# A fused attention and spectral-mixing kernel: the last loop gets one PSUM bank per z tile, a new order of steps, other modes for its pairs, the batch ends at places 15 and 16, and a second store queue

## The chip, the core and the metric

The kernel runs on one core of a Trainium2 chip. The core has a matrix engine (TensorE, PE in the profile; PEld are its weight loads), VectorE (DVE), ScalarE (ACT), GpSimd (POOL) and SyncE (SP). Each takes its own instructions in program order; they meet through semaphores. TensorE writes its sums to PSUM, eight banks of 128 partitions by 512 fp32 values; results leave through ACT or DVE to SBUF, and go to memory by DMA. The metric is the device time of one execution in microseconds (us), the median over several runs.

## The reference

```
scores = q k^T / 8 + min(-(cum_i - cum_j), 0), causal;  cum = cumsum(max(s, 0))
attn = softmax(scores) v                       # 8 batches, 8 heads, 576 x 64
x = heads side by side                         # 8 x 576 x 512
X = rfft(x, axis=1);  Y[m] = X[m] (w_r + i w_i)[m]   # the first 64 modes, each 512 x 512
u = x + irfft(Y, n=576)
out = u + max(u @ w_ch, 0)                     # 8 x 576 x 512, fp32
```

## The kernel before

A first stage computes attention for one head pair and batch after the other, then the forward transform of its result as matrix products (`fft`), while the mode weights stream in through GpSimd's DMA queue. A second stage (`modes`, called for eight chunks `c` of eight modes each) multiplies the modes; each chunk gives `yb`, the spectral rows y, and with `w_ch` the rows `vb` = y w_ch. Because u = x + G y (G is the inverse transform), the product u w_ch is x w_ch + G (y w_ch). So `yv` holds, for each batch, the 128 spectral rows (16 for each chunk) of both kinds: `which` = 0 for y, 1 for y w_ch. A small DMA (`spread`, L491, on SP's queue) moves the rows of the last two chunks to their places in `yv`. The last chunk's rows are the last to arrive.

The last loop forms the output. Its unit is a pair of row tiles of 128 x 512 values: `pairs` lists 18 of them, 16 ordinary pairs (b, T), (b, T + 1) and two pairs of **batch ends**, the last 64 rows of each batch, four batches in a pair, two tiles of two times 64 rows. Before, these stand at places 2 and 4. For each pair two sums are formed in PSUM, each of two banks:

- u: step X (`add_x`, L749) puts x into it through an identity matrix, step U (`add_u`, `add_y`, L721) adds G y.
- z: step Z (`add_z`, `add_y`, L721) puts in G (y w_ch). The product x w_ch was made and kept in SBUF earlier (`z1s`), for all but the first two pairs. How it joins z is the pair's mode in `ways`: "s", ACT copies it into PSUM first (step S, `seed`, L872); "e", it is kept as two fp16 digits and added by four matmuls (step E, L878); "v", DVE adds it (step K, L784); "g", ACT copies z to SBUF and GpSimd adds it there (both in step R, L769 and L770). In the other modes R is ACT's relu from PSUM to the result tile `r_w` (L774).
- step F (`finish`, L792 or L794), on DVE, adds max(z, 0) and u, and issues the store on SP's queue (L796; for batch ends two stores of 64 partitions each, L801).

The z tiles come from `zpool`, two buffers of two banks; the u tiles from two pools, one for even and one for odd pairs. So X of pair i waits for F of pair i - 2, and a new z tile waits until both banks of the tile two before are read. All of it is scheduled by hand: the string of steps near the end is the order in which the instructions are emitted, and each engine takes its own in that order. Pairs 0 and 1 (`NPRE`) have their z nearly complete before the loop: chunk 6 and 7 are added with `add_last`, which takes y w_ch of one chunk straight from `vb`, with a matrix `Gx_sb` that holds that chunk's rows of G at the partitions of batch 0, and doesn't wait for the `spread`. For other pairs Z reads all 128 rows of `yv`.

```
if ways.get(i) == "g":
    nc.scalar.copy(out=rs[i], in_=zs[i])
    nc.gpsimd.tensor_tensor(out=rs[i], in0=rs[i], in1=z1s[i], op=ALU.add)
```

Of the kernel before, what the change touches and what calls it, by code (L numbers as in the profile page):

```python
# [18 lines left out]
def kernel(  # L19
# [60 lines left out]
    G_np = G_np.reshape(P, SP).astype(np.float16)  # L80
# [24 lines left out]
    G_sb = gp.tile([P, SP], FP16, name="G_sb")  # L105
# [391 lines left out]
    for i, b in ((2, 0), (4, B // 2)):  # L497
        pairs.insert(i, ((b, NF), (b + 2, NF)))
# [4 lines left out]
    ways = dict(zip(kept, "evgvggeggsgsgsgs"))  # L503
# [85 lines left out]
    zpool = ctx.enter_context(tc.tile_pool(name="z_psum", bufs=2, space=PSUM))  # L589
# [33 lines left out]

    def x_times_wch(i, last):
        zs[i] = z = zpool.tile([P, 2, DM], FP32, name="z_ps", tag="z")
        for x in range(2):
            for dt in range(DT):
                nc.tensor.matmul(  # L628
                    z[:, x, :], xts[i][:, x, dt, :], wch_sb[:, dt, :],
# [3 lines left out]
    def keep(i):  # L633
# [7 lines left out]
        keep_product(i, slice(0, 2), zs.pop(i))  # L641
# [72 lines left out]
    x_pool = ()  # L714
    GK = P - 2 * MC * NX

    def add_y(dst, i, which, rows=slice(0, P), start=False):

        for x, (b, T) in enumerate(pairs[i]):
# [7 lines left out]
    def add_last(dst, i, yb, cols=slice(0, DM), c=NX - 1):  # L727

        for x, (b, T) in enumerate(pairs[i]):
            nc.tensor.matmul(  # L730
                dst[x][:, cols], Gx_sb[:, c, bass.ts(T, P)], yb[:, cols],
                start=False, stop=True, skip_group_check=True,
            )
# [31 lines left out]
    def relu(i):  # L765

        rs[i] = result(i)
        if ways.get(i) == "g":
            nc.scalar.copy(out=rs[i], in_=zs[i])  # L769
            nc.gpsimd.tensor_tensor(out=rs[i], in0=rs[i], in1=z1s[i], op=ALU.add)  # L770
            return
        n = 1 if i in (0, last) else 2
        for x in range(0, 2, n):
            nc.scalar.activation(out=rs[i][:, x : x + n], in_=zs[i][:, x : x + n], func=ACTF.Relu)  # L774
        if i in x_pool:
            b, T = pairs[i][0]
            r = rs[i].rearrange("p x (g d) -> p x g d", d=P)
            nc.gpsimd.tensor_tensor(
                out=r, in0=r, in1=x_all[:, :, b, T : T + 2, :].rearrange("p g t d -> p t g d"), op=ALU.add
            )  # L780

    def kept_sum(i):
        rs[i] = result(i)
        nc.vector.tensor_tensor(out=rs[i], in0=zs[i], in1=z1s[i], op=ALU.add)  # L784

# [148 lines left out]
```

## Time and profile before

| | |
|---|---|
| median of 4 runs | 446.97 us (446.69 to 447.4) |
| the profiled execution | 447.04 us, its span 445.1 us |
| granted TensorE clock, mean | 0.912 |
| bytes written to memory | 9.44 MB |

The page cuts the span into 40 slices and gives for each the busy tenths of every engine and of the DMA engines. The last loop is the end of it:

| window, us | PE | DVE | ACT | POOL | DMA share | GB/s |
|---|---|---|---|---|---|---|
| 400 to 410 | 8.90 | 2.34 | 0.58 | 0.00 | 0.75 | 150 |
| 410 to 420 | 9.48 | 6.98 | 5.08 | 1.07 | 0.36 | 131 |
| 420 to 430 | 9.91 | 8.30 | 8.60 | 10.00 | 0.95 | 316 |
| 430 to 440 | 8.56 | 9.09 | 6.99 | 7.65 | 1.03 | 398 |
| 440 to 446 | 0.00 | 0.58 | 0.00 | 0.00 | 0.55 | 210 |

The columns are busy microseconds of each engine in the window, the mean busy share of the 16 DMA engines (which can come out a little over 1), and the rate at which they moved data. The last mode weights land at 408.5 us and the last matmul on them (L456) starts at 408.58 us; the first relu of the loop (L774) starts at 412.61 us. Of one execution's rows, these are the durations in the loop: two matmuls of 512 columns 0.59 us, and a matmul every 0.2155 us where many follow each other; an ACT step on 1024 columns 1.02 us (L769, L774, L872), on 512 columns 0.594 us; a DVE step on 1024 columns 1.22 us (L792, L794), on 512 columns 0.683 us; GpSimd's sum on 1024 columns (L770) 2.37 us.

### The profile page before, as it was taken

How to read it: one execution, taken by the hardware profiler on the slowest of the kernel's cores; microseconds unless marked ns; L12 is line 12 of the kernel's file. 1: busy time of each engine (PE TensorE's matmuls, PEld its weight loads, DVE VectorE, ACT ScalarE, POOL GpSimd, SP SyncE). 2: the span in 40 equal slices, each digit the busy share in tenths (PEclk: the TensorE clock that was granted, in tenths of full speed). 3: DMA queues.
4: the chain of work that ended last, by engine and by line, in shares of the span. 5: the costliest groups of instructions: out<-in, count | busy, mean ns of one | idle time of the engine just before them, and what ended most of it. 6: DMA issues, size and time to landing. Idle time of an engine off the chain costs nothing.

```text
span 445.1 us, 11399 instructions
## 1 busy us (share of the span) xinstructions
PE 341.0 (77%) x4697; PEld 217.2 (49%) x4729; DVE 251.2 (56%) x574; ACT 221.1 (50%) x387; POOL 243.0 (55%) x375
## 2 busy tenths in 40 slices
PE   1688998995909599892498759399987997768994
PEld 1366665563606365661366436256664555433341
DVE  7766766672605366671266527157765564451785
ACT  1576787464606375671256525256661244321593
POOL 7766656565556566455565546464644443530393
PEclk9998999996967889997579969889999799989998
DMA  9999999999999999999999999999999999996598
GB/s 181 201 207 206 204 206 204 208 206 207 207 209 202 206 202 183 205 206 208 207 202 206 208 207 203 209 206 203 203 210 209 211 210 209 209 217 133 179 351 334
DMA packets 72675, 93.30 MB, mean 210 GB/s; under 512 B 29664, under 2 KB 31200, under 8 KB 72624
## 3 DMA queue, kind: packets, MB, share of 16 engines
q0 software_dynamic: 63408, 81.29, 104.2%
q1 hardware_dynamic: 9216, 11.29, 7.8%
q8 instruction: 37, 0.61, 0.5%
q14 instruction: 14, 0.11, 0.1%
HBM read 163.51 MB, written 9.44 MB: 389 GB/s over the span
## 4 chain that ended last, share of the span: by engine, by line
DMA 55%; PE 22%; POOL 6%; DVE 6%; issue 5%; ACT 3%; POOLq 1%; DVEq 0%
DMA w_sb<-in_moe_w_r_dram 20%; DMA qk<-in_k_dram 19%; DMA w_sb<-in_moe_w_i_dram 14%; PE z_ps L628 4%; PE yp L456 4%; PE sc_ps L378 3%; POOL r_w L770 3%; PE tr_ps L336 3%; POOL w_sb L232 2%; PE sc_ps L372 2%; DMA x_all<-in_moe_w_r_dram 2%; ACT p_sb L386 1%; PE ft_ps L433 1%; PE av_ps L407 1%; PE xt_ps L618 1%
## 5 line engine op out<-in xcount | busy, mean ns | idle before, releaser
L386 ACT ACTIVATE p_sb<-sc_ps,cumt_sb 128x576 f16<-128x576 f32 (+1 forms) x256 | 141.6, 636 | 50.2 <-PE sc_ps L378 49.8
L232 POOL DMA_DIRECT2D w_sb<-in_moe_w_r_dram x120 | 71.2, 594 | 62.0 <-DMA w_sb<-in_moe_w_r_dram 17.0
L232 POOL DMA_DIRECT2D w_sb<-in_moe_w_i_dram x120 | 71.1, 594 | 62.1 <-DMA w_sb<-in_moe_w_i_dram 19.2
L340 DVE COPY qt<-tr_ps 64x576 bf16<-64x576 bf16 x64 | 47.8, 747 | 75.3 <-PE tr_ps L336 75.3
L336 PE MATMUL tr_ps<-ident,qk 64*64 64x64 bf16 x1152 | 34.9, 204 | 65.1 <-DMA qk<-in_k_dram 27.5
L378 PE MATMUL sc_ps<-qt,kt 128*128 128x64 bf16 (+2 forms) x352 | 69.9, 306 | 4.2 <-ACT kt L340 2.2
L232 POOL DMA_DIRECT2D v<-in_v_dram x72 | 52.1, 724 | 34.7 <-DMA w_sb<-in_moe_w_i_dram 10.0
L336 PEld LDWEIGHTS <-qk 64*64 64x64 bf16 x1152 | 26.5, 117 | 75.3 <-DMA qk<-in_k_dram 28.6
L372 PE MATMUL sc_ps<-negm,ident 128*128 128x256 bf16 x256 | 53.9, 295 | 0.2
L378 PEld LDWEIGHTS <-kt 128*128 128x128 bf16 x384 | 40.1, 105 | 26.2 <-issue 5.0
L357 ACT ACTIVATE p<-sc_ps,cumt 128x64 f16<-128x64 f32 x32 | 10.0, 314 | 72.1 <-PE sc_ps L353 72.1
L456 PE MATMUL yp<-w_sb,xs 128*32 128x512 bf16 (+1 forms) x480 | 38.6, 407 | 9.1 <-DMA w_sb<-in_moe_w_i_dram 2.6
L407 PE MATMUL av_ps<-v,p_sb 128*128 128x65 f16 x1024 | 43.3, 195 | 0.1
L407 PEld LDWEIGHTS <-p_sb 128*128 128x128 f16 x1024 | 37.7, 99 | 4.8 <-DVE x_all L417 1.9
L443 DVE CAST xs<-ft_ps 64x128 bf16<-64x128 f32 x128 | 31.4, 284 | 7.0 <-PE ft_ps L433 6.2
L412 DVE TENSOR_REDUCE den<-av_ps 128x5 f32<-128x10 f32 x64 | 10.8, 169 | 41.4 <-PE av_ps L407 40.4
L433 PE MATMUL ft_ps<-Ff_sb,x_all 128*64 128x96 f16 (+1 forms) x640 | 32.3, 220 | 1.0 <-DVE x_all L417 1.0
L417 DVE TENSOR_TENSOR x_all<-av_ps,rcp 128x320 f16<-128x320 f32 x64 | 31.4, 491 | 2.2
L456 PEld LDWEIGHTS <-xs 128*32 128x32 bf16 (+1 forms) x512 | 19.3, 145 | 23.3 <-issue 9.5
L340 ACT COPY kt<-tr_ps 64x576 bf16<-64x576 bf16 x32 | 23.0, 719 | 15.2 <-DVE qt L340 14.6
L433 PEld LDWEIGHTS <-x_all 128*64 128x64 f16 (+1 forms) x640 | 22.0, 111 | 8.8 <-DVE x_all L417 1.1
L628 PE MATMUL z_ps<-wch_sb,xs 128*128 128x512 f16 x96 | 24.9, 406 | 0.2 <-DVE xs L622 0.2
(111 smaller groups left out, 425.5 us busy)
## 6 DMA issues: line engine op xcount, KB each, us to landing
w_sb<-in_moe_w_r_dram POOLq DMA_DIRECT2D x120, 256.0 KB, 8.8
w_sb<-in_moe_w_i_dram POOLq DMA_DIRECT2D x117, 256.0 KB, 8.7
out_dram<-r_w SPq DMA_DIRECT2D x14, 512.0 KB, 3.2
v<-in_v_dram POOLq DMA_DIRECT2D x72, 64.0 KB, 7.4
qk<-in_q_dram POOLq DMA_DIRECT2D x15, 288.0 KB, 7.9
qk<-in_k_dram POOLq DMA_DIRECT2D x15, 288.0 KB, 9.2
x_all<-in_moe_w_i_dram POOLq DMA_DIRECT2D x6, 256.0 KB, 7.5
out_dram<-r_w SPq DMA_DIRECT2D x6, 256.0 KB, 3.2
```

What stands on the lines that cost most here:

```text
L232: nc.gpsimd.dma_start(out=dst, in_=src)
L336: nc.tensor.transpose(ps[rows, r, :], src[rows, r, :], ident16[rows, rows])
L340: copy(out=to[:, :, :, half * RH : half * RH + RH], in_=ps[HP * i : HP * i + HP].rearrange("d r (h p) -> d h p r", h=2),)
L372: nc.tensor.matmul(ps[:, bass.ds(w * S, W)], ident16, negm[:, bass.ts(r, W)], start=True, stop=False, skip_group_check=True,)
L378: nc.tensor.matmul(ps[:, c0 : c0 + i1 - i0], keys[:, w, r, :], qh[:, i0:i1], start=False, stop=True, skip_group_check=True,)
L386: nc.scalar.activation(out=pt[:, poff[x] : poff[x] + S - w * W], in_=ps[:, w * S : (w + 1) * S - w * W], func=ACTF.Exp, bias=cumt_sb[:, x, ...
L407: nc.tensor.matmul(ps[:, I, r : r + NCH], lhsT, rhs, start=(i == 0), stop=(i == len(todo) - 1), skip_group_check=True,)
L417: nc.vector.tensor_tensor(out=x_all[:, g, b, :, D * h : D * h + D], in0=ps[:, :, 1 : NCH], in1=rcp.unsqueeze(2).to_broadcast([P, NT, D]), ...
L433: nc.tensor.matmul(ps[HP * h : HP * h + HP, q_, :], x_all[:nT, g, b, T, q_::2], Ff_sb[:nT, T, 3 * HM * h : 3 * HM * (h + 1)], start=(T == ...
L443: nc.vector.tensor_copy(out=xs[g % 2][rows, :, k, h, :, b, :], in_=ps[rows, :, k * HM : (k + 2) * HM].rearrange("p q (r m) -> p q r m", r=2),)
L456: nc.tensor.matmul(ps[32 * cg : 32 * cg + 32, :], cols[k0:, q_, 1 - ri, :, c * MC // 2 + cg], wt[(g, c, ri, cg // 2)][k0:, 2 * (cg % 2) + ...
L628: nc.tensor.matmul(z[:, x, :], xts[i][:, x, dt, :], wch_sb[:, dt, :], start=(dt == 0), stop=(last and dt == DT - 1), skip_group_check=True,)
```

## The change

It touches the last loop, what leads to it, and which pair is handled where:

- z tiles are one bank each, named by the parity of the pair and the half: four tags with one buffer each. The steps S, E, Z, R and K are given for one half ("a" or "b"), and GpSimd's sum becomes a step of its own, G, also by halves. X, U and F stay whole, but F of pairs 0 and 17 is given by halves.
- The batch ends move to places 15 and 16. Pairs 2 to 14 are now ordinary pairs.
- `ways` changes: "g" holds for eight pairs as before (now 2, 4, 8, 10, 11, 13, 15, 17), "v" for 3 and 5 as before, "e" for one pair (7) in place of two, "s" for five (6, 9, 12, 14, 16) in place of four.
- Pair 2 (batch 1) is `direct`: its Z takes 112 rows from `yv`, and the last chunk's 16 rows from `vb` through a new matrix `Gy_sb`, which has that chunk's rows of G at the partitions of batch 1. `Gy_sb` is cleared by DVE and loaded by SP once, beside `Gx_sb`.
- Of each pair of batch ends the first store goes to SP's queue in F, the second to ACT's queue in a step D of its own.
- For pairs 0 and 1 the last chunk's sums are ordered by column halves first, then by pairs.
- `G_sb` is 576 columns wide in place of 640.
- The order of all steps is a new one.

```diff
--- before.py
+++ after.py
...
-    G_np = G_np.reshape(P, SP).astype(np.float16)
+    G_np = np.ascontiguousarray(G_np.reshape(P, SP)[:, :S].astype(np.float16))
...
-    G_sb = gp.tile([P, SP], FP16, name="G_sb")
+    G_sb = gp.tile([P, S], FP16, name="G_sb")
...
     pairs = [((b, T), (b, T + 1)) for b in range(B) for T in range(0, NF, 2)]
-    for i, b in ((2, 0), (4, B // 2)):
+    for i, b in ((15, 0), (16, B // 2)):
         pairs.insert(i, ((b, NF), (b + 2, NF)))
...
-    ways = dict(zip(kept, "evgvggeggsgsgsgs"))
+    ways = dict(zip(kept, "gvgvsegsggsgsgsg"))
...
-    zpool = ctx.enter_context(tc.tile_pool(name="z_psum", bufs=2, space=PSUM))
+    Gy_sb = finpool.tile([P, 2 * P], FP16, name="Gy_sb")
+    nc.vector.memset(Gy_sb.bitcast(FP32), 0.0)
+    nc.sync.dma_start(out=Gy_sb[1:P:B], in_=d_Gx[:, NX - 1, : 2 * P])
+    zpool = ctx.enter_context(tc.tile_pool(name="z_psum", bufs=1, space=PSUM))
...
+    def start_z(i, x):
+        zs[i, x] = zpool.tile([P, DM], FP32, name="z_ps", tag=f"z{i % 2}{x}")
+
     def x_times_wch(i, last):
-        zs[i] = z = zpool.tile([P, 2, DM], FP32, name="z_ps", tag="z")
         for x in range(2):
+            start_z(i, x)
             for dt in range(DT):
                 nc.tensor.matmul(
-                    z[:, x, :], xts[i][:, x, dt, :], wch_sb[:, dt, :],
+                    zs[i, x], xts[i][:, x, dt, :], wch_sb[:, dt, :],
                     start=(dt == 0), stop=(last and dt == DT - 1), skip_group_check=True,
...
-        keep_product(i, slice(0, 2), zs.pop(i))
+        for x in range(2):
+            keep_product(i, x, zs.pop((i, x)))
...
+    direct = (2,)
...
-    def add_y(dst, i, which, rows=slice(0, P), start=False):
-
-        for x, (b, T) in enumerate(pairs[i]):
+    def add_y(dst, i, which, rows=slice(0, P), start=False, xx=(0, 1)):
+
+        for x in xx:
+            b, T = pairs[i][x]
             for r, bb, _ in parts(b, T):
                 nc.tensor.matmul(
...
-    def add_last(dst, i, yb, cols=slice(0, DM), c=NX - 1):
-
-        for x, (b, T) in enumerate(pairs[i]):
+    def add_last(dst, i, yb, cols=slice(0, DM), c=NX - 1, xx=(0, 1)):
+
+        for x in xx:
+            b, T = pairs[i][x]
             nc.tensor.matmul(
-                dst[x][:, cols], Gx_sb[:, c, bass.ts(T, P)], yb[:, cols],
+                dst[x][:, cols], Gy_sb[:, bass.ts(T, P)] if b else Gx_sb[:, c, bass.ts(T, P)], yb[:, cols],
...
-    def relu(i):
-
-        rs[i] = result(i)
+    def relu(i, x):
+
+        if i not in rs:
+            rs[i] = result(i)
         if ways.get(i) == "g":
-            nc.scalar.copy(out=rs[i], in_=zs[i])
-            nc.gpsimd.tensor_tensor(out=rs[i], in0=rs[i], in1=z1s[i], op=ALU.add)
-            return
-        n = 1 if i in (0, last) else 2
-        for x in range(0, 2, n):
-            nc.scalar.activation(out=rs[i][:, x : x + n], in_=zs[i][:, x : x + n], func=ACTF.Relu)
-        if i in x_pool:
-            b, T = pairs[i][0]
-            r = rs[i].rearrange("p x (g d) -> p x g d", d=P)
-            nc.gpsimd.tensor_tensor(
-                out=r, in0=r, in1=x_all[:, :, b, T : T + 2, :].rearrange("p g t d -> p t g d"), op=ALU.add
-            )
-
-    def kept_sum(i):
-        rs[i] = result(i)
-        nc.vector.tensor_tensor(out=rs[i], in0=zs[i], in1=z1s[i], op=ALU.add)
-
-    def finish(i):
-        n = 1 if i in (0, last) else 2
+            nc.scalar.copy(out=rs[i][:, x], in_=zs[i, x])
+        else:
+            nc.scalar.activation(out=rs[i][:, x], in_=zs[i, x], func=ACTF.Relu)
+
+    def gpsimd_sum(i, x):
+
+        r = rs[i][:, x]
+        if ways.get(i) == "g":
+            nc.gpsimd.tensor_tensor(out=r, in0=r, in1=z1s[i][:, x], op=ALU.add)
+        else:
+            b, T = pairs[i][x]
+            r = r.rearrange("p (g d) -> p g d", d=P)
+            nc.gpsimd.tensor_tensor(out=r, in0=r, in1=x_all[:, :, b, T, :], op=ALU.add)
+
+    def kept_sum(i, x):
+        if i not in rs:
+            rs[i] = result(i)
+        nc.vector.tensor_tensor(out=rs[i][:, x], in0=zs[i, x], in1=z1s[i][:, x], op=ALU.add)
+
+    def finish(i, x=None):
+        xx = slice(0, 2) if x is None else slice(x, x + 1)
         b, T = pairs[i][0]
-        for x in range(0, 2, n):
-            o, u = rs[i][:, x : x + n, :], us[i][:, x : x + n, :]
-            if ways.get(i) in ("v", "g"):
-                nc.vector.scalar_tensor_tensor(out=o, in0=o, scalar=0.0, in1=u, op0=ALU.max, op1=ALU.add)
-            else:
-                nc.vector.tensor_tensor(out=o, in0=u, in1=o, op=ALU.add)
-            if T < NF:
-                nc.sync.dma_start(
-                    out=out[b, bass.ds((T + x) * P, n * P), :].rearrange("(x p) e -> p x e", p=P), in_=o
-                )
+        o, u = rs[i][:, xx, :], us[i][:, xx, :]
+        if ways.get(i) in ("v", "g"):
+            nc.vector.scalar_tensor_tensor(out=o, in0=o, scalar=0.0, in1=u, op0=ALU.max, op1=ALU.add)
+        else:
+            nc.vector.tensor_tensor(out=o, in0=u, in1=o, op=ALU.add)
         if T == NF:
-            for r, bb, _ in parts(b, T):
-                nc.sync.dma_start(
-                    out=out[bb : bb + 3 : 2, NF * P :, :].rearrange("x t e -> t x e"), in_=rs[i][r]
-                )
+            store_tails(nc.sync, i, 0)
+        else:
+            n = 2 if x is None else 1
+            nc.sync.dma_start(
+                out=out[b, bass.ds((T + (x or 0)) * P, n * P), :].rearrange("(x p) e -> p x e", p=P), in_=o
+            )
+
+    def store_tails(queue, i, y):
+        b, T = pairs[i][0]
+        r, bb, _ = parts(b, T)[y]
+        queue.dma_start(out=out[bb : bb + 3 : 2, NF * P :, :].rearrange("x t e -> t x e"), in_=rs[i][r])
 
     def z_of(i):
-        return [zs[i][:, x, :] for x in range(2)]
+        return [zs[i, x] for x in range(2)]
...
-    for i in range(NPRE):
-        for cols in halves:
+    for cols in halves:
+        for i in range(NPRE):
             add_last(z_of(i), i, vb, cols)
...
-    def start_z(i):
-        zs[i] = zpool.tile([P, 2, DM], FP32, name="z_ps", tag="z")
-
-    def seed(i):
-        start_z(i)
-        nc.scalar.copy(out=zs[i], in_=z1s[i])
-
-    def digits(i):
-        start_z(i)
-        for x in range(2):
-            for y in range(2):
-                nc.tensor.matmul(
-                    zs[i][:, x, :], ident16h, z1s[i][:, y, x, :],
-                    start=(y == 0), stop=False, skip_group_check=True,
-                )
-
-    def add_z(i):
-        if i not in zs:
-            start_z(i)
-        add_y(z_of(i), i, 1, start=ways[i] in ("v", "g"))
+    def seed(i, x):
+        start_z(i, x)
+        nc.scalar.copy(out=zs[i, x], in_=z1s[i][:, x])
+
+    def digits(i, x):
+        start_z(i, x)
+        for y in range(2):
+            nc.tensor.matmul(
+                zs[i, x], ident16h, z1s[i][:, y, x, :], start=(y == 0), stop=False, skip_group_check=True,
+            )
+
+    def add_z(i, x):
+        start = (i, x) not in zs
+        if start:
+            start_z(i, x)
+        z = {x: zs[i, x]}
+        if i in direct:
+            add_y(z, i, 1, slice(0, P - 2 * MC), start=start, xx=(x,))
+            add_last(z, i, vb, xx=(x,))
+        else:
+            add_y(z, i, 1, start=start, xx=(x,))
 
...
     steps = {
-        "S": seed, "E": digits, "Z": add_z, "R": relu, "K": kept_sum, "X": add_x, "U": add_u, "F": finish,
+        "S": seed, "E": digits, "Z": add_z, "R": relu, "G": gpsimd_sum, "K": kept_sum, "X": add_x, "U": add_u,
+        "F": finish, "D": lambda i: store_tails(nc.scalar, i, 1),
     }
     for step in (
-        "R0 X1 F0 U1 R1 E2 F1 Z2 Z3 R2 X2 K3 U2 Z4 F2 X3 R4 Z5 U3 K5 Z6 X4 R6 U4 F3 Z7 E8 R7 F4 Z8 X5 R8 "
-        "Z9 U5 R9 X6 F5 U6 Z10 S11 F6 X7 U7 R10 Z11 F7 X8 R11 U8 Z12 F8 X9 S13 U9 X10 R12 F9 Z13 U10 R13 "
-        "Z14 F10 X11 U11 S15 F11 X12 R14 U12 Z15 F12 X13 R15 U13 Z16 F13 X14 R16 U14 X15 F14 S17 U15 F15 "
-        "X16 U16 Z17 F16 X17 R17 U17 F17 "
+        "R0a X1 R0b U1 F0a R1a Z2a F0b Z2b R1b R2a X2 F1 U2 R2b G2a Z3a Z3b K3a Z4a Z4b R4a X3 G2b K3b Z5a "
+        "R4b U3 K5a S6a Z5b G4a S6b F2 E7a Z6a Z6b R6a G4b Z7a F3 X4 R6b U4 R7a Z8a K5b Z8b S9a X5 F4 U5 "
+        "R8a E7b R8b G8a Z7b F5 Z9a R7b X6 U6 R9a G8b Z10a S9b F6 X7 R10a U7 Z9b S12a G10a Z10b F7 X8 R9b "
+        "U8 R10b Z11a F8 Z11b S12b X9 G10b U9 R11a Z12a R11b F9 X10 G11a R12a U10 Z12b S14a Z13a F10 X11 "
+        "G11b R12b U11 R13a Z13b Z14a S14b F11 X12 G13a R14a U12 R13b Z14b Z15a F12 R14b X13 G13b U13 R15a "
+        "Z15b S16a X14 G15a F13 R15b U14 S16b Z16a Z17a R16a Z17b G15b F14 Z16b X15 R17a U15 R16b G17a X16 "
+        "R17b F15 U16 G17b F16 X17 D15 U17 F17a D16 F17b "
     ).split():
-        steps[step[0]](int(step[1:]))
+        i = int(step[1:].rstrip("ab"))
+        if step[-1] in "ab":
+            steps[step[0]](i, "ab".index(step[-1]))
+        else:
+            steps[step[0]](i)
```

## The prediction

> **What bounds the kernel now.** I read the page's slices first, then the chain of waits, then the last loop in the timeline and in windows of half a microsecond.
>
> ```profile
> POOL 7766656565556566455565546464644443530393
> DMA  9999999999999999999999999999999999996598
> GB/s 181 201 207 206 204 206 204 208 206 207 207 209 202 206 202 183 205 206 208 207 202 206 208 207 203 209 206 203 203 210 209 211 210 209 209 217 133 179 351 334
> ```
>
> For 36 of 40 slices the DMA engines are full with weights. The change leaves those bytes alone (`G_sb` is 128 bytes shorter in each partition: nothing), so I count the start of the loop as unmoved: the weight stream ends it at 408.6 us, and modes reordered behind it are hidden by the stream. Only slices 37 to 40 can change. There, the timeline of before (start, duration, engine, instruction, the idle time before it and what ended it):
>
> ```profile
> 415.10 1.16 PE L721 MATMUL z_ps<-yv,G_sb 128*64 128x512 f16 x6 [0.34 <-DMA yv<-v_sb]
> 418.71 1.35 SPq L801 DMA_DIRECT2D out_dram<-r_w  x2
> 418.93 2.37 POOL L770 TENSOR_TENSOR r_w<-r_w,r_sb 128x1024 f32<-128x1024 f32 x1 [20.18 <-ACT r_w L769]
> 421.26 14.17 POOL L770 TENSOR_TENSOR r_w<-r_w,z 128x1024 f32<-128x1024 f32 x6
> 430.62 1.22 DVE L792 SCALAR_TENSOR_TENSOR r_w<-r_w,u_ps 128x1024 f32<-128x1024 f32 x1 [0.52 <-POOL r_w L770]
> 439.30 1.28 DVE L794 TENSOR_TENSOR r_w<-u_ps,r_w 128x512 f32<-128x512 f32 x2
> ```
>
> GpSimd's first sum starts only at 418.93, because the first Z that reads `yv` waits for the spread until 415.10. From then GpSimd has hardly a gap: 8 x 2.37 = 18.96 us. DVE waits for it, last before the row at 430.62, which is F10 (the order of DVE's rows is the order of the F and K steps). The windows show what the chain of waits doesn't:
>
> ```profile
> 419.50:420.00 0.50, 0.50 (x5) 0.14 (x4) 0.50 (x2) 0.34 (x1) 0.50 (x1) 1.00 0.00 0
> 420.00:420.50 0.50, 0.50 (x6) 0.14 (x4) 0.50 (x2) 0.50 (x1) 0.50 (x1) 1.00 0.85 197
> 420.50:421.00 0.50, 0.50 (x6) 0.21 (x3) 0.50 (x1) 0.18 (x1) 0.50 (x1) 1.00 0.99 197
> 421.00:421.50 0.50, 0.50 (x4) 0.19 (x2) 0.32 (x2) 0.20 (x1) 0.50 (x2) 1.00 0.89 193
> 421.50:422.00 0.50, 0.50 (x4) 0.23 (x3) 0.50 (x1) 0.50 (x1) 0.50 (x1) 1.00 1.03 365
> ...
> 432.50:433.00 0.50, 0.50 (x4) 0.22 (x3) 0.48 (x1) 0.48 (x1) 0.41 (x1) 1.00 0.59 225
> 433.00:433.50 0.50, 0.50 (x4) 0.27 (x3) 0.49 (x1) 0.07 (x1) 0.44 (x1) 1.00 1.08 422
> ...
> 442.50:443.00 0.50, 0.00 (x0) 0.00 (x0) 0.00 (x0) 0.00 (x0) 0.00 (x0) 0.50 1.06 414
> 443.00:443.50 0.50, 0.00 (x0) 0.00 (x0) 0.00 (x0) 0.00 (x0) 0.00 (x0) 0.50 0.18 66
> ```
>
> The last three columns are clock, DMA share, GB/s. From 433 on the store engines are full, at about 406 GB/s: one pair (524,288 bytes) takes **1.29 us**. F10 ends at 431.84, its data flow 0.9 us later (432.75), and eight pairs are left: 432.75 + 8 x 1.29 = 443.07, where the windows show the data end at about 443.1. So the end is GpSimd, then F10, then **the stores**, not DVE's last row at 440.58; 2.0 us of landing and closing work follow to 445.1. A pair of batch ends is dear: from 420.05 it moves at 195 GB/s with full engines, then at 365, and 0.524 MB are through at about 422.15: **2.1 us** a pair. Summed over the windows, 0.29 MB are gone at 421.5, so the first half (64 partitions) takes 1.35 us and the second less.
>
> **The change, part by part.**
>
> **Direct pair 2 and the new order.** PE runs X1 and U1 from 412.73 (4 x 0.2155), then Z2 from 413.59, with no landing to wait for; the 0.34 us of PE at 415.10 goes. ACT takes R0 and R1 by halves from 412.5 (4 x 0.49, the step between two 512-column rows in sequence), then R2a to 415.1: GpSimd starts at 415.2 in place of 418.93. Pair 2's four added matmuls (0.86 us) stand where PE waited; the four of the lost "e" (0.86) go. What is late next: the sums themselves.
>
> **GpSimd by halves.** No row shows 512 columns. Below: half of 2.37, 1.19. Above: 1.6, if a fixed 0.8 us is in each. The Trainium skill (GPSIMD Engine Reference, section "Elementwise — side-by-side cycle accounting") gives 4.497 us for 2048 columns; with the row of 2.37 for 1024 a straight line gives 2.08 ns a column and 0.24 fixed, so I take the estimate 1.30. 16 x 1.30 = 20.8 against 18.96: by the row alone the halves are free, by the rule they cost 1.8 us of the 3.7 gained.
>
> **ACT and DVE.** ACT's halves: 0.98 a pair against 0.92 to 1.04 between whole rows, so nothing; one more seed is 0.98, inside the 1.4 us that ACT was idle between 420 and 430 (8.60 busy of ten). DVE: K by halves 4 x 0.61 against 2 x 1.22, nothing. F stays whole for 16 pairs.
>
> **Walking the new list.** I gave every step the durations above (PE 0.2155 a matmul and 0.375 for the last to come out; batch ends 0.5 for each four; DVE 1.16 in sequence; 0.04 to 0.09 from one engine to the next) and each engine its steps in order. The old list so walked has F10 ending at 432.00 (trace: 431.84) and F17 at 440.83 (trace: 440.58), so 0.2 is to be taken off. The new list: F4 421.9, F9 428.1, F13 433.7, F14 434.9, F15 436.5, F17b 438.9. F15 starts when U15's matmuls are out (X15 and U15, 1.0 us, behind Z16b), just after GpSimd's G15b. DVE ends **1.9 us earlier**.
>
> **Stores.** Fourteen ordinary pairs go first. F4's data can flow at 422.7, and eleven pairs (4 to 14) need 14.2 us: 436.9. So the queue is empty when F15 ends at 436.3 (436.5 less 0.2). The batch ends need about 1.3 us from issue to data (418.71 to 420.05): **437.65**. Left are two pairs of batch ends and pair 17, 1.29: the end of data is 437.65 + 2p + 1.29, p the time for one pair of batch ends. It equals the 443.1 of before at **p = 2.08**. D15 and D16 stand on ACT behind its last relu (R17b, 435.5), so nothing waits behind them; SP issues T15, T16, F17a, F17b in order and is free each time.
>
> **What two queues do for p.** Before, one after the other on SP, p is 2.1 (the row). If the halves fill each other's gaps, p is 1.29, the rate of a full tile. The Trainium skill speaks against it (SBUF — State Buffer, section "Can I just issue two DMAs to hit both halves?"): two concurrent DMAs on partitions 0 and 64 came out only 6% faster than in turn, since they share the same engines. With the first half's 1.35 for each this is 2.7 / 1.06 = 2.55, which the row of 2.1 already beats without a second queue. The trace has the second half partly at 365 GB/s, so the upper half isn't held to half the rate, and could pass while the lower waits. Nearest is the lower half alone, 1.35; I take **p = 1.5**, between it and the row, with 1.29 and 2.55 kept for the range.
>
> Sum: 437.65 + 3.0 + 1.29 = 441.94; less 443.1 is -1.16. 447.04 - 1.16 = 445.88 for the profiled execution; the median stands 0.07 below that execution, so **445.8**.
>
> **What was at nothing.** `Gy_sb`'s clear and load stand beside `Gx_sb`'s (0.485 us of DVE at 341.3, 0.498 of SP after it), 60 us before their first use, hidden by the weights; uncovered, half a microsecond each. The halves first order in `add_last` brings pair 1's z no later. F0a starts 0.07 earlier: it moves no store that binds.
>
> **Rivals** (0.2%, 0.9 us, is what a measurement can tell from none).
>
> - *B, the second queue brings nothing*: p = 2.1, data end 437.65 + 4.2 + 1.29 = 443.14: **447.0**. For it: the full engines at 195 GB/s. Then the DVE gain is eaten by batch ends moved from a place where stores had slack (0.00 at 419.50) to one with none.
> - *C, slower: the halves hinder each other at the end.* Both at the first half's rate, or a little worse as packets alternate: p = 2.8, end 444.54, +1.44: **448.4**. It decides from p = 2.08 on and shows over 0.2% from 2.5; the skill's rule lies at that edge. For it: at their new place nothing but pair 17 lies behind them. Against: the 365.
> - *D, GpSimd's halves are dear.* At 1.45 the walk has F15 1.1 us later (445.8 becomes 446.9), at 1.6 2.5 us later: **448.3**. Against: its six rows in a row took 2.36 each, with no gap between them.
>
> **Chances.** The forecast A 0.52, of which 0.06 fall within 0.2%; its own range is 444.8 to 446.6. B 0.15, all within. C 0.21, 0.03 of it within. D 0.12, slower. Faster 0.46, same 0.24, slower 0.30. The range: below, p = 1.29 and F15 0.4 early, 444.8 (-1.0); above, C, 448.4.
>
> **What would show it.** GpSimd's first sum before 416; its halves at 1.3; DVE's last row near 438.7; no full store engines at 437; from 437.6 the batch ends at over 300 GB/s with two queues active; data end at 442. Wrong: batch ends near 200 GB/s again, or DVE idle behind GpSimd after 430 for over 2 us, or the weights' end moved from 408.6.

## The result and the profile after

The changed kernel takes 448.16 us (median of 43 runs, 446.52 to 450.19), the kernel before 447.32 (64 runs on the same chips, 445.73 to 449.23 but for one of 953.85): ratio **1.0016, 95% interval 1.0008 to 1.0024**. It is slower by 0.7 us (0.4 to 1.1), which is inside the 0.2% that the prediction called no different, and not faster by 1.2 us as forecast. The profiled execution took 448.46 us, its span is 446.5.

These are the rows of the changed kernel's page that the prediction read of the kernel before, and a new queue q10, ScalarE's, with 288 packets:

```profile
POOL 6756665555556665545566546465554443530692
...
DMA  9999999999999999999999999999999999995697
GB/s 181 202 207 205 204 202 205 206 203 207 207 209 199 203 207 180 206 207 208 207 203 206 208 207 202 208 207 204 207 210 209 211 210 209 209 218 116 220 378 260
...
q10 hardware_dynamic: 288, 0.52, 0.4%
```

In the last two slices the stores move 378 and then 260 GB/s, where before it was 351 and 334: the end of the kernel has become the poorer part. The granted TensorE clock, 0.902 on average in this execution and 0.912 in the one of before, has no part in it: from 410 to 438 us it is 1.00 in both. The timeline of the changed kernel (start, duration, engine, instruction, idle time before it and what ended it):

```profile
415.96 2.51 POOL L788 TENSOR_TENSOR r_w<-r_w,r_sb 128x512 f32<-128x512 f32 x2 [17.16 <-DMA yv<-v_sb]
...
433.07 2.50 POOL L788 TENSOR_TENSOR r_w<-r_w,xs 128x512 f32<-128x512 f32 x2
...
435.19 0.62 PE L759 MATMUL u_ps<-x_all,ident16h 64*64 64x512 f16 x4
...
435.74 0.62 PE L730 MATMUL u_ps<-yv,G_sb 128*64 128x512 f16 x4
...
436.46 1.22 DVE L804 SCALAR_TENSOR_TENSOR r_w<-r_w,u_ps 128x1024 f32<-128x1024 f32 x1 [0.97 <-POOL r_w L788]
...
437.71 1.75 SPq L818 DMA_DIRECT2D out_dram<-r_w  x2
437.72 1.92 ACTq L818 DMA_DIRECT2D out_dram<-r_w  x2
...
438.86 1.28 DVE L804 SCALAR_TENSOR_TENSOR r_w<-r_w,u_ps 128x512 f32<-128x512 f32 x2
439.57 3.01 SPq L811 DMA_DIRECT2D out_dram<-r_w  x2
```

The last modes' matmuls started at 409.42 in this execution, 0.84 later than in the one shown of before. To compare, 0.84 is taken off every time of this execution; "in before's time" says that this was done. In before's time GpSimd starts at 415.12 and DVE's last row ends at 439.30: the loop's engines did become faster, DVE by 1.3 us (440.58 before). At 437.7, and again at 438.85, both queues issue at the same moment. What the stores make of it is in the windows (the last three columns are clock, DMA share, GB/s):

```profile
438.50:439.00 0.50, 0.26 (x2) 0.00 (x0) 0.47 (x2) 0.00 (x0) 0.00 (x0) 1.00 0.51 180
439.00:439.50 0.50, 0.00 (x0) 0.00 (x0) 0.50 (x2) 0.00 (x0) 0.00 (x0) 1.00 0.88 213
439.50:440.00 0.50, 0.00 (x0) 0.00 (x0) 0.50 (x2) 0.00 (x0) 0.00 (x0) 1.00 1.04 217
440.00:440.50 0.50, 0.00 (x0) 0.00 (x0) 0.14 (x1) 0.00 (x0) 0.00 (x0) 1.00 0.89 197
440.50:441.00 0.50, 0.00 (x0) 0.00 (x0) 0.00 (x0) 0.00 (x0) 0.00 (x0) 1.00 1.00 299
...
444.00:444.50 0.50, 0.00 (x0) 0.00 (x0) 0.00 (x0) 0.00 (x0) 0.00 (x0) 0.50 0.64 242
444.50:445.00 0.50, 0.00 (x0) 0.00 (x0) 0.00 (x0) 0.00 (x0) 0.00 (x0) 0.50 0.14 53
```

At 439 the engines are nearly full and move 213 GB/s, the sign that the prediction had named for being wrong. By the trace's packets SP's first batch-end store flows from 439.0, and all but one of its completion packets come from 440.33 to 440.6; ScalarE's, issued in the same moment, has its first packet at 440.33. Two pairs of batch ends and pair 17 take from 439.05 to about 444.65, **5.6 us for 1.57 MB**; a few last packets end at 444.95, as in the kernel before, where the data end at about 443.1 and a few last packets at 443.55. With 1.29 for pair 17, p = (5.6 - 1.29) / 2 = **2.15 us** (2.11 with the 1.39 that a pair takes at this kernel's 378 GB/s), the 2.1 of one queue in the kernel before. No compute engine works after 440.2.

### The profile page after: what moved, and what is told of

Read it like the earlier page. It is cut to its first block, busy times and chain, and to the rows that moved or that the text cites. A ratio compares the mean times of both kernels' runs of the same rounds, so it can differ in the third digit from the quotient of the medians.

```text
span 446.5 us, 11440 instructions
## 1 busy us (share of the span) xinstructions
PE 343.8 (77%) x4695; PEld 219.2 (49%) x4727; DVE 250.0 (56%) x576; ACT 224.3 (50%) x417; POOL 244.4 (55%) x383
## 4 chain that ended last, share of the span: by engine, by line
DMA 59%; PE 27%; DVE 5%; issue 4%; POOL 3%; ACT 0%; DVEq 0%; POOLq 0%
DMA w_sb<-in_moe_w_r_dram 21%; DMA w_sb<-in_moe_w_i_dram 20%; DMA qk<-in_k_dram 10%; PE yp L456 5%; PE z_ps L634 4%; PE av_ps L407 2%; PE sc_ps L378 2%; PE ft_ps L433 2%; DMA x_all<-in_moe_w_r_dram 2%; PE tr_ps L336 2%; PE sc_ps L372 2%; DMA x_all<-in_moe_w_i_dram 2%; DMA y_acc<-in_moe_w_r_dram 2%; POOL w_sb L232 2%; DMA qk<-in_q_dram 2%
## 5 line engine op out<-in xcount | busy, mean ns | idle before, releaser
L336 PE MATMUL tr_ps<-ident,qk 64*64 64x64 bf16 x1152 | 36.2, 208 | 64.3 <-DMA qk<-in_k_dram 29.3
L336 PEld LDWEIGHTS <-qk 64*64 64x64 bf16 x1152 | 27.6, 120 | 74.9 <-DMA qk<-in_k_dram 30.4
L433 PE MATMUL ft_ps<-Ff_sb,x_all 128*64 128x96 f16 (+1 forms) x640 | 34.2, 230 | 1.0 <-DVE x_all L417 1.0
L433 PEld LDWEIGHTS <-x_all 128*64 128x64 f16 (+1 forms) x640 | 23.3, 117 | 9.4 <-DVE x_all L417 1.1
L340 DVE COPY kt<-tr_ps 64x576 bf16<-64x576 bf16 x32 | 24.4, 762 | 0.4
```

Of the source, the lines that this page charges most:

```text
L336: nc.tensor.transpose(ps[rows, r, :], src[rows, r, :], ident16[rows, rows])
L340: copy(out=to[:, :, :, half * RH : half * RH + RH], in_=ps[HP * i : HP * i + HP].rearrange("d r (h p) -> d h p r", h=2),)
L433: nc.tensor.matmul(ps[HP * h : HP * h + HP, q_, :], x_all[:nT, g, b, T, q_::2], Ff_sb[:nT, T, 3 * HM * h : 3 * HM * (h + 1)], start=(T == ...
```

## The experiments

Each ratio is to the kernel before, run beside it on the same chip, with its 95% interval. The profiles were compared by where the time of the stores goes. This table is worked out from the packet records of the traces: "lead" is from the start of the last modes' matmuls to the first store packet, "stores" from the first to the last packet; of that, "none" is the time without any packet in flight, "packets" their summed time over 16 engines, and "some" the rest, in which a part of the engines is idle. All in us.

```
kernel              lead   stores   none   packets   some
before              6.23   28.74    2.53   25.48     0.73
before_again        6.22   28.40    2.55   25.48     0.37
changed             6.11   29.43    2.10   26.19     1.14
after_again         6.11   29.31    2.10   26.17     1.03
one_queue           6.11   29.65    2.09   26.25     1.31
before_narrow       6.22   29.43    2.39   26.38     0.66
after_aligned       6.11   29.29    2.31   25.32     1.66
one_queue_aligned   6.11   29.56    2.30   25.29     1.97
ends_3_5_aligned    6.12   29.21    2.73   25.75     0.73
before_ends_late    6.23   30.78    3.28   25.21     2.29
halves_mid          6.23   31.55    2.53   26.84     2.18
stores_full         6.11   28.93    2.14   25.67     1.12
```

The lead hardly moves. What differs is the time of the stores, between 28.4 and 31.6 us; the two profiles of one kernel differ in it by 0.1 to 0.3 us. From before to changed the stores take 0.6 to 1.0 us more and the lead 0.1 less, which agrees with the 0.7 us of the result.

**The two kernels again**, for a second profile of each.

> The kernel before once more, for a second profile on the chip of the other runs. In the two profiles shown the last mode weights land at 408.54 us before and at 409.38 us after, and full stores run at 406 GB/s before and about 380 after. Theory L (the change itself delays the end of the weights): here again 408.5 and 406. Rival N (both differences are those of one execution or one chip): here anywhere between 408.3 and 409.6, and the store rate as in the changed kernel beside it. Time within 0.1% of the kernel before.

> The changed kernel once more. Theory L: weights end at 409.4 us again, 0.8 us behind the run of the kernel before beside it. Rival N: no fixed difference. Both: GpSimd's first sum 6.5 us after the weights' end, DVE's last row 30.7 us after it (32.0 in the kernel before), the two pairs of batch ends at 2.15 us each. Ratio 1.0016.

0.9992 (0.9979 to 1.0005) and 1.0015 (1.0003 to 1.0027). The second profile of before has its last modes at 407.52, over 1 us earlier than the first, and its stores last 28.40 us; that of the changed kernel repeats its first one within 0.15 us.

**One queue in the changed kernel.**

```diff
             store_tails(nc.sync, i, 0)
+            store_tails(nc.sync, i, 1)
...
-        "R17b F15 U16 G17b F16 X17 D15 U17 F17a D16 F17b "
+        "R17b F15 U16 G17b F16 X17 U17 F17a F17b "
```

> The changed kernel with both halves of each pair of batch ends stored on SP's queue, right behind each other, and no store on ACT's queue. Theory B (the second queue brings nothing, the halves pass one after the other either way): p stays 2.1 to 2.2 us, the time within 0.3 us of the changed kernel. Rival Q1 (the second queue does help): about 1 us slower than the changed kernel. Rival Q2 (the second queue hurts: its first data flowed 2.6 us after its issue in place of 1.3, and the last two stores on SP took 1.4 us each to issue): 0.5 to 1 us faster.

1.0024 (1.0014 to 1.0034). The ratios differ by 0.4 us in favour of two queues, and those of the same pair of kernels with aligned tiles (below) by 0.8 us; neither difference is clear of its noise, and in the profiles the stores with one queue take 0.2 to 0.3 us longer. So the second queue may bring a little, but not the 1.2 us that p = 1.5 in place of 2.1 would be.

**The batch ends early in the new loop.** The edit of one_queue, and:

```diff
-    for i, b in ((15, 0), (16, B // 2)):
+    for i, b in ((3, 0), (5, B // 2)):
```

> The changed kernel with the batch ends at places 3 and 5, both halves on SP's queue; steps and modes as in the changed kernel, so that only the pairs' places and the stores' queue differ. Theory P (the batch ends' slow stores were moved from where stores had slack to where they have none): about 1 us faster than the changed kernel and faster than the kernel before by 0.2 to 0.5 us; data of the stores end about 3.3 us after DVE's last row, not 4.5. Rival (the place doesn't matter, the later start does): no faster than the changed kernel.

1.0016 (1.0006 to 1.0027), as the changed kernel. Away from the end of the loop the batch ends cost as much.

**The 128 bytes.** In the new loop `G_sb` has 576 columns in place of 640, and so each tile allocated behind it starts 128 bytes earlier: the first weight and result tile at byte 97,664 of a partition, not at 97,792 = 382 x 256. First that alone in the kernel before:

```diff
-    G_np = G_np.reshape(P, SP).astype(np.float16)
+    G_np = np.ascontiguousarray(G_np.reshape(P, SP)[:, :S].astype(np.float16))
...
-    G_sb = gp.tile([P, SP], FP16, name="G_sb")
+    G_sb = gp.tile([P, S], FP16, name="G_sb")
```

> The kernel before with one part of the change alone: G_sb 576 columns wide in place of 640. That puts every tile allocated after it 128 bytes lower in each partition, so the weight tiles and the result tiles r_w, whose addresses were multiples of 256, lie 128 bytes off one (97664 in place of 97792). Theory A (a store of 2048-byte rows from addresses off 256 bytes is slower: 88 ns a packet in the four runs with the narrow G_sb, 84.0 in the two of before): 87 to 91 ns a packet here, the stores about 5% slower and the time 0.6 to 1.2 us longer. Rival (the slower packets come of the new loop, its second queue or its busier engines): 84.0 ns, and no change of time.

**1.0029 (1.0016 to 1.0041)**, +1.3 us (0.7 to 1.8) from a line that the prediction had put at nothing; in the profiles 0.7 to 1.0 us of it are in the stores. Over the stretch where the stores fill the engines, first before, then before_narrow:

```profile
434.00:442.00 8.00, 4.85 (x21) 1.84 (x19) 6.23 (x7) 3.48 (x5) 3.79 (x2) 1.00 1.05 407
```

```profile
434.00:442.00 8.00, 4.80 (x21) 1.84 (x19) 6.18 (x7) 3.42 (x5) 3.73 (x2) 1.00 1.02 378
```

The engines are full in both, at 407 and at 378 GB/s. In this stretch every packet of 2,048 bytes takes 84 ns in the first; in the second the mean is 87.8, while over half of the packets still take 84 and the longest 134. The Trainium skill (DMA: Bandwidth & Descriptors, section "How a descriptor splits into AXI transactions") says that a transfer which doesn't start at a multiple of 256 bytes begins with a transaction at the boundary below it, and that the unused bytes still cost beats of 32 bytes. Counted as in its table, 2,048 bytes that start 128 off take 68 beats for 64, an estimate of 6% more for every packet. The runs show 4.6% more on average, but not on every packet, so the page's rule has the direction, and whether it is the cause is not shown.

Then the tiles of the changed kernel put back on multiples of 256, by moving `G_sb` behind them; and the same with one_queue and with ends_3_5:

```diff
-    G_sb = gp.tile([P, S], FP16, name="G_sb")
...
+    gpool = ctx.enter_context(tc.tile_pool(name="g_sb", bufs=1))
+    G_sb = gpool.tile([P, S], FP16, name="G_sb")
```

> The changed kernel, G_sb still 576 columns, but allocated behind the weight tiles, so that the weight and result tiles lie at multiples of 256 again (96512 onward); nothing else differs. Theory A: 84.0 ns a packet, data of the stores end about 1 us sooner after DVE's last row, the time about 1 us shorter than the changed kernel's, so about 0.2 us below the kernel before. Rival: no change.

> As after_aligned, with both halves of the batch ends on SP's queue. Theory B (the halves pass one after the other on two queues as on one): within 0.3 us of after_aligned. Rival Q1 (the second queue helps): 0.5 to 1 us slower.

> As after_aligned, with the batch ends at places 3 and 5 and all stores on SP. Theory P (at the end the batch ends' stores are bare, earlier they are partly hidden): 0.3 to 0.8 us faster than after_aligned, and about 0.7 us faster than the kernel before. Rival (the stores are the bound from the first on, so a pair of batch ends costs its 2.1 us anywhere): as after_aligned.

1.0013 (1.0000 to 1.0027), 1.0031 (1.0017 to 1.0045) and 1.0017 (1.0005 to 1.0028). The packets of after_aligned are back at 84.4 ns, 0.87 us less in sum (25.32 against 26.19), but "some" grows by 0.52 and "none" by 0.21: behind the last ordinary pair, F14, the faster stores are through sooner and the engines wait for the batch ends. So the 128 bytes cost 1.3 us where the stores hardly wait, and here nothing that these runs can tell.

**The places alone, in the old loop.**

```diff
-    for i, b in ((2, 0), (4, B // 2)):
+    for i, b in ((15, 0), (16, B // 2)):
```

> The loop of before, and of the change only the places of the two batch-end pairs: 15 and 16, all stores on SyncE's queue. Theory E (the end of the loop is set by the stores, and a batch-end pair costs p = 2.15 us of data, wherever it stands): the two pairs moved from the start of the loop to its end keep their 4.3 us, so the sum of data stays the same, but pair 2 is now an ordinary pair and its store can begin at once; ratio 1.000, 0.998 to 1.002. Theory F (at the end of the loop their price lies bare, 2 x (2.15 - 1.29) = 1.7 us, while at the start it lay beside waits for VectorE): ratio 1.004, 1.002 to 1.006. Theory S (the later start of the last mode's matmuls in the changed kernel, 409.1 on average of seven profiles against 408.2 of three, comes with the new order of the pairs and not with the new loop): that start at 409.0 to 409.6 here, against 407.5 to 408.6 if it comes from elsewhere.

**1.0063 (1.0040 to 1.0085)**, more than each theory gave; its profile has the stores 2.0 us longer (30.78 for 28.74). Windows of before_ends_late at the end:

```profile
440.00:441.00 1.00, 1.00 (x7) 0.49 (x6) 0.84 (x1) 0.32 (x1) 0.04 (x1) 1.00 1.04 406
441.00:442.00 1.00, 0.46 (x3) 0.00 (x0) 0.83 (x2) 0.76 (x2) 0.00 (x0) 1.00 0.73 184
442.00:443.00 1.00, 0.00 (x0) 0.00 (x0) 0.84 (x2) 0.00 (x0) 0.00 (x0) 1.00 0.95 231
443.00:444.00 1.00, 0.00 (x0) 0.00 (x0) 0.00 (x0) 0.00 (x0) 0.00 (x0) 1.00 1.01 356
444.00:445.00 1.00, 0.00 (x0) 0.00 (x0) 0.00 (x0) 0.00 (x0) 0.00 (x0) 1.00 0.78 242
```

The rate falls from 406 to 184 as the first batch end comes, and to 242 for the second pair. "some" is 1.56 above before, mostly here, and "none" 0.75, which lies early in the loop: the trace has no packet in flight for 0.82 us at 422.8 and for 0.67 at 426.5. The changed kernel has the same places and is 2.1 us better (1.0063 - 1.0016 = 0.0047 of 447, by the two intervals 1.0 to 3.2): that much the rest of the change won, and the places had taken more.

**The shape alone: ordinary pairs 9 to 12 cut the same way**, in the kernel before.

```diff
-                nc.sync.dma_start(
-                    out=out[b, bass.ds((T + x) * P, n * P), :].rearrange("(x p) e -> p x e", p=P), in_=o
-                )
+                for rr in (slice(0, P // 2), slice(P // 2, P)) if 9 <= i <= 12 else (slice(0, P),):
+                    nc.sync.dma_start(
+                        out=out[b, bass.ds((T + x) * P, n * P), :].rearrange("(x p) e -> p x e", p=P)[rr],
+                        in_=o[rr],
+                    )
```

> The loop of before, with the stores of the ordinary pairs 9, 10, 11 and 12 each cut into the partitions 0 to 63 and 64 to 127, both on SyncE's queue, one behind the other; these lie in the saturated stretch. Theory H (the shape is what costs: a store from half the partitions pays 2.15 us for a pair where a whole one pays 1.29): 4 x 0.86 = +3.4 us, ratio 1.0077, 1.005 to 1.010. Theory T (it is the batch ends alone that are dear, by what stands ahead of them or by their places in the output): ratio 1.000, within 0.001. In between, some +1.3 us (1.003), if only the first half of each that finds the queue empty is slow.

**1.0051 (1.0034 to 1.0068)**: 2.3 us, 0.57 a pair by the times, and 0.70 by the stores of its profile (31.55 - 28.74 = 2.81). That is less than the 0.86 (2.15 - 1.29) that a batch end costs above an ordinary pair. Windows of halves_mid in what was a stretch at about 400:

```profile
431.00:432.00 1.00, 0.72 (x4) 0.26 (x3) 1.00 (x2) 1.00 (x2) 1.00 (x1) 1.00 1.02 297
432.00:433.00 1.00, 1.00 (x6) 0.47 (x5) 0.97 (x2) 0.94 (x1) 0.86 (x1) 1.00 0.95 231
433.00:434.00 1.00, 1.00 (x7) 0.41 (x6) 1.00 (x1) 0.62 (x1) 0.98 (x1) 1.00 0.70 215
434.00:435.00 1.00, 1.00 (x6) 0.49 (x5) 0.93 (x2) 0.78 (x2) 1.00 (x1) 1.00 1.03 363
435.00:436.00 1.00, 0.92 (x6) 0.33 (x4) 0.93 (x2) 1.00 (x2) 0.67 (x2) 1.00 0.60 188
```

These pairs have nothing of a batch end but its stores of 64 partitions, and their rate falls to about 200 GB/s in the same way. So most of the price, 0.57 to 0.70 of 0.86, is the shape's, and no place or queue that was tried took it away.

**Another cut of the same bytes.** If 64 partitions are dear, 128 may be cheap: two stores for a pair again, each of 128 partitions x 2 KB to two batches. In the kernel before, and the same edit in the changed kernel (after_by_x), with the tiles at multiples of 256 (aligned_by_x) and in stores_full (stores_full_by_x):

```diff
-            for r, bb, _ in parts(b, T):
-                nc.sync.dma_start(
-                    out=out[bb : bb + 3 : 2, NF * P :, :].rearrange("x t e -> t x e"), in_=rs[i][r]
-                )
+            for x in range(2):
+                nc.sync.dma_start(out=out[b + 2 * x : b + 2 * x + 2, NF * P :, :], in_=rs[i][:, x, :])
```

> The kernel before, where each batch-end pair is stored in two stores of 128 partitions x 2 KB (batches b and b+1, then b+2 and b+3) in place of two of 64 partitions x 4 KB. Theory H (a store of 64 partitions is the price): each pair falls from 2.15 to 1.29 us, and as the loop is bound by its stores, both count: 2 x 0.86 = -1.7 us, ratio 0.9962, 0.995 to 0.998. Theory T (the tails are dear by their places in the output): 1.000, within 0.001. Rival W (early in the loop the stores wait for VectorE, and what the pairs at places 2 and 4 save becomes idle time of the queue): 0.9985 to 1.000, with packets of 84 ns at the tails all the same.

> The changed kernel, its two batch-end pairs at places 15 and 16 stored by batches (128 partitions x 2 KB) on the same two queues. Theory H: the pairs lie bare at the end, 5.6 us of data from 439.05 become 4 x 0.69 + 1.29 = 4.0 us (at the 380 GB/s of the unaligned tiles), -1.6 us: 446.5 us, ratio 0.9982, 0.997 to 0.9995, just what the forecast of 445.8 us with p = 1.5 or less would have needed. Theory T: 1.0016 as the changed kernel, within 0.001. Rival Q (two queues are slow together whatever the shape): between, 1.000 to 1.001, the data of ScalarE's queue again 2.5 us after their issue.

> The same, and the weight-stage tiles at multiples of 256 bytes. Theory H: 0.1 to 0.4 us below after_by_x, ratio 0.9975, 0.996 to 0.999; the whole gain that was forecast for the change then shows. Theory T: 1.0013. If it beats before_by_x, the new loop is worth something once its stores are free; if before_by_x beats it, the new loop is worth nothing.

> The third order (batch ends at places 2 and 4 of the half-grain loop, all on SyncE's queue, tiles at multiples of 256 bytes), its ends stored by batches. Theory H: -1 to -1.7 us from its 1.0020, ratio 0.9970 to 0.9998; with the queue full from 426 us on, a gain of the early pairs counts only as far as the stores behind them are ready. Theory T: 1.002 as it was.

All four expectations missed by far: 1.036 (1.0334 to 1.0387), 1.0396 (1.0370 to 1.0422), 1.039 (1.0364 to 1.0416) and 1.0364 (1.0339 to 1.0390), some 16 to 18 us slower. Windows of before_by_x behind such a store:

```profile
426.00:428.00 2.00, 2.00 (x10) 0.88 (x9) 1.93 (x2) 1.89 (x2) 2.00 (x2) 1.00 0.13 51
428.00:430.00 2.00, 1.93 (x10) 0.83 (x9) 1.40 (x3) 1.09 (x2) 2.00 (x2) 1.00 0.13 51
```

A DMA share of 0.13 is 2 engines of 16, at 51 GB/s, and in these windows no other store passes beside it. The trace's completion packets say the same: 296 in the loop where before has 352, 14 fewer for each of the four stores. The Trainium skill (DMA: Bandwidth & Descriptors, section "Why a DMA increments its semaphore by 16 and not by 1") has the rule: the number of engines is the largest up to 16 that divides the slowest dimension of both sides; the output side here has 2 batches. The idea was bad for a reason that the page states, and it tests nothing of the 64 partitions.

**The order of the two halves**, in the kernel before and in the changed kernel.

```diff
-            for r, bb, _ in parts(b, T):
+            for r, bb, _ in parts(b, T)[::-1]:
...
-        r, bb, _ = parts(b, T)[y]
+        r, bb, _ = parts(b, T)[1 - y]
```

> The kernel before, with the two stores of each batch-end pair in the other order: partitions 64 to 127 first, then 0 to 63. Theory L (the lower partitions are the slow ones): the first store's packets take 84 ns and the second's 150. Theory O (the first of the two is slow, whichever it is): 150 first, then 84. Time in both: as before, ratio 1.000, within 0.002, since both stores together take 2.15 us.

> The changed kernel with the same swap: SyncE's queue takes partitions 64 to 127 of each batch-end pair, ScalarE's 0 to 63. Theory Q (one queue's stores wait for the other's, whatever they hold): 5.6 us of data for the two pairs and F17 as in the changed kernel, ScalarE's data 2.5 us after issue, ratio 1.0016, 1.000 to 1.003. Theory L with queues that run beside each other: SyncE's half goes out at 84 ns within 0.7 us of its start and ScalarE's slow half runs beside the next pair's, -0.5 us, ratio 1.0005.

1.0001 (0.9984 to 1.0019) and 1.0018 (1.0002 to 1.0034): no change in either. Windows of before_swapped, whose first store now holds partitions 64 to 127:

```profile
422.00:422.50 0.50, 0.50 (x5) 0.11 (x2) 0.50 (x1) 0.36 (x1) 0.50 (x1) 1.00 0.96 205
422.50:423.00 0.50, 0.50 (x3) 0.20 (x2) 0.34 (x1) 0.01 (x1) 0.50 (x2) 1.00 0.97 172
423.00:423.50 0.50, 0.50 (x4) 0.26 (x3) 0.49 (x1) 0.50 (x1) 0.50 (x1) 1.00 0.97 316
```

The first is slow, whichever half it is: the first 128 packets of such a pair, one store's worth, take 160 ns on average (159 in the kernel before), the next 128 take 91. In after_swapped, where the two stores have queues of their own, SP's first 128 packets take some 150 ns, and ScalarE's data again start when SP's end.

**A third order of the steps**, made for stores without gaps: batch ends back at places 2 and 4, one queue, tiles at multiples of 256, no direct pair.

```diff
-    for i, b in ((15, 0), (16, B // 2)):
+    for i, b in ((2, 0), (4, B // 2)):
...
-    ways = dict(zip(kept, "gvgvsegsggsgsgsg"))
+    ways = dict(zip(kept, "svgvgegsggsgsgsg"))
...
-    direct = (2,)
+    direct = ()
...
+        "R0a X1 U1 F0a R0b F0b X2 R1a R1b S2a Z2a Z3a S2b F1 K3a Z2b U2 R2a R2b Z4a Z4b Z3b R4a R4b F2 Z5a "
...
```

> The changed kernel's half-grain loop with another order of steps: the two batch-end pairs back at places 2 and 4, all stores on SyncE's queue, first and last pair by halves, both spectral halves of pair 2 seeded by ScalarE, and the weight-stage tiles at addresses that are multiples of 256 bytes. Theory E (the sum of store data, and the idle time of the store queue, decide): the order leaves no idle time between the first store and the last except before F2, the data end 0.5 to 1.3 us earlier after the start of the last mode's matmuls than in the changed kernel (34.1 to 34.9 against 35.4), ratio against before 0.997 to 0.9995. Rival (each order that is planned on paper meets waits that the plan doesn't know): 1.001 to 1.004.

1.0020 (1.0005 to 1.0035): no better. From 427 to 443 it moves 400 GB/s without a gap, but its stores last 28.93 us in all: the two batch ends come at 420 and 424, at 195 and 188 GB/s in their first microsecond, the first of them behind 1.5 us without a packet. No version here beats the kernel before.

## Why the prediction was wrong

**The mechanism of the first half was right.** GpSimd starts at 415.12 (415.2 forecast), its halves take 1.26 to 1.28 us (1.30 was the estimate from the Trainium skill's GPSIMD Engine Reference, section "Elementwise — side-by-side cycle accounting", and the measurement lies a little below it: the halves cost 2.5 a pair where a whole row cost 2.37), DVE ends earlier, and the store engines are half idle before the batch ends (a share of 0.51 from 438.5 to 439.0). The forecast for DVE, 1.9 us earlier, came out as 1.3.

**The step that failed is p = 1.5**, the time for one pair of batch ends on two queues. It measured 2.15, as on one queue before (one_queue's profile, 5.9 us for the same data, gives 2.3): 2 x 0.65 = 1.3 us in the sum. The choice rested on the 365 GB/s of the second half, read as "the upper half isn't held to half the rate". The swap shows that it isn't the upper half that is fast but the second, and the trace shows that the second queue's data start only when the first's end (both at 440.33), so the halves do not fill each other's gaps. The right reading lay in the row itself: 2.1 for one pair, taken as it stands. The Trainium skill's rule that was weighed there (SBUF — State Buffer, section "Can I just issue two DMAs to hit both halves?") had the direction right, and the 2.55 estimated from it lies above the 2.15 measured. Rival B had this mechanism; its time, no change, is 0.7 us too low, and that is the next step.

**F15 was 0.54 us late**, the second step that failed: it ends at 436.84 in before's time (436.3 forecast). Its row says that it waited for GpSimd. But in the trace's own time GpSimd's sums for it were done at 435.57 (the row at 433.07), and X15 and U15 end at 436.36, just before F15 starts at 436.46. So it was PE, as the prediction had it. X15 began about where the walk has it (434.35 in before's time). From there X15 and U15 took 1.17 us for the 1.0 given, F15 1.22 for 1.16, and the 0.2 taken off the walk was not there to take. PE has no idle time that could make up for such delays: before, then the changed kernel, from 425 to 435:

```profile
425.00:435.00 10.00, 9.62 (x44) 4.17 (x43) 9.19 (x9) 8.83 (x10) 9.86 (x5) 1.00 1.00 382
```

```profile
425.00:435.00 10.00, 10.00 (x48) 3.87 (x46) 9.09 (x9) 9.68 (x20) 9.43 (x8) 1.00 1.02 378
```

PE went from 9.62 busy to 10.00 of 10, GpSimd (the last of these columns before the clock) from 9.86 to 9.43: the new order relieved one full engine and filled another.

**The sum.** With 437.65 + 0.55 for the start of the batch ends' data and 5.6 for 4.29 the end of data is 443.8 in before's time, against 443.1: +0.7, where -1.16 was forecast and the ratio says +0.7. The two steps, 1.3 and 0.55, are the whole difference.

**"`G_sb` ... nothing" was wrong in kind.** The bytes are nothing, the addresses behind them are not: 1.3 us in the old loop. It didn't decide this case, since after_aligned is no faster than the changed kernel by more than the noise.

**The start of the loop as unmoved** holds as far as can be told. Single profiles put the start of the last modes' matmuls anywhere from 407.5 to 410.5, with a mean of 408.8 for seven of the old loop and of 409.0 for twelve of the new one; before_swapped has 410.26 in its profile and a median that is no slower. The 0.84 us between the two profiles shown is such scatter.

**Three slips of the working** changed little. Pair 2 has four matmuls in its Z where an ordinary pair has two, so two were added (0.43 us) and not four. By the prediction's own sum the eleven pairs end at 436.9, so the queue is empty then and not already at 436.3; the batch ends' data, at 437.65, are behind both. The lower end of the range, with p = 1.29 and F15 0.4 early, is -0.8 and not -1.0.

**The batch ends at a place "where stores had slack".** Rival B said that the gain is eaten by moving them to one without, and before_ends_late shows that move at 2.8 us (1.8 to 3.8). Yet ends_3_5 and stores_full, with the batch ends early in the new loop, don't get it back: their stores take 28.9 to 29.6 us (before: 28.74), with 2.1 to 2.7 us without a packet (before: 2.53). Why the new loop gains 2.1 us with late batch ends and nothing with early ones was not taken apart.

**What stays open**: why the first of two 64-partition stores runs at half rate and the second doesn't, why the second queue's data start so late, and why at a shifted address only some packets take longer.

## What to carry to other kernels

Where stores fill the DMA engines, the end of the loop is the first store plus the sum of their data and their gaps; take an odd-shaped transfer at its own measured time, and don't divide that by a second queue or another place before a run shows it. A tile that is made smaller moves the addresses of all that is allocated behind it: look where the tiles that are stored then start (128 bytes off a multiple of 256 cost 1.3 us in one of these loops and nothing that could be told in the other). And read how many of the 16 engines a transfer will use from its outermost dimension before its shape is changed: an output of two batches had two.

## What was not expected of the hardware

- 128 bytes off a multiple of 256, store packets of 2,048 bytes take 87.8 ns on average instead of 84.0, though over half still take 84, and the stores move 378 GB/s instead of 407.
- Of two stores of 64 partitions issued one after the other, the first runs at some 160 ns a packet and the second at 91, whichever half of the partitions comes first.
- Two queues that issue such stores in the same moment (437.71 and 437.72) have data from 439.0 and from 440.33, and SP's next two issues of ordinary stores take 1.35 and 1.57 us where 0.37 is usual. Behind the same four stores on one queue they take 0.81 and 1.06.
- A store whose output side has an outermost dimension of 2 runs on 2 engines: 51 GB/s, 16 us for two such pairs.
